# A new written order from the third batch on, other engines for movable operations, and squares taken from one SBUF copy

## The chip, the core and the metric

The kernel runs on one core of a Trainium2 chip. The core has TensorE (PE in the rows; its weight loads are PEld), VectorE (DVE), ScalarE (ACT), GpSimd (POOL) and SyncE (SP, which only starts transfers here). The metric is the device time of one execution in microseconds (us), as the median of several runs. "Slower" and "faster" are meant in this time.

## The reference

Cut to what matters:

```python
# attention: x (8, 8, 512, 64), state (8, 8, 32, 64)
scores  = scale * x @ state.T;   a  = softmax(scores)
xread   = a @ state
scores2 = scale * state @ x.T;   a2 = softmax(scores2)
sread   = a2 @ x
attn    = concatenate([xread, sread], axis=2)        # (8, 8, 544, 64)
# feed-forward on tokens of width 512, d_ff = 2048
h   = maximum(attn_as_tokens @ w_in, 0)
out = (h * h) @ w_out
```

Everything is float32. There are 8 batches of 512 read tokens and one last group of 256 tokens (the `sread` rows of all batches).

## The kernel before, in words

**Precision.** TensorE multiplies rounded float32 (`F32R`). Each operand is split into a rounded part (`hi`, made by ScalarE) and a remainder (`lo`, a subtraction), and a product is three matmuls: hi·hi, hi·lo, lo·hi.

**Blocks.** Block 0 to 7 is a batch, block 8 the `sread` tokens. For each block, `hidden(blk, fc)` computes 128 of the 2048 hidden features for all tokens into a PSUM bank `ph` (two banks in all), and `accumulate(blk, fc)` multiplies the squared result into four PSUM banks `acc`. Between the two, ScalarE and VectorE make `g_hi` and `g_lo` of the squared relu. A PSUM bank `ph` is free again only when `g_lo` has been made from it, so TensorE can wait twice for a late `g_lo`: in `accumulate`, which reads it, and in the hidden step two further on, which needs the bank.

The weights of `hidden` are not `w_in` but `w_in` already multiplied with the batch's `state` (`w2`). They are computed in rows of small matmuls (`w2ps`, `w4ps`), and scores (`st`) and reads (`pr`) stand in such rows too. For the last two batches `last_w2` splits `w2ps` into `w2h` (ScalarE) and `w2l` (VectorE). The softmax of each batch gives `k_hi`, `k_lo`.

**Blocks 5 to 7** use a product with seven instead of eight multiplications (`hidden_fast`, `accumulate_fast`, keys `fast.blk.p.h`). It needs sums of four quarters of the squares. Each step makes: `f_sum` (128x256), `d_sum` (128x256), `e_sum` (128x128), and the remainders `p_lo`, `f_lo` (tiles `a_g_lo`, 128x256) and `b_lo` (tile `b_g_lo`, 128x384). These are the small additions. `add_weights` (key `sums.p`) makes the matching sums of `w_out` (tiles `v`, `sv`, `one`, `both`, `first`); it runs beside the end of block 8 and all of block 5.

**What sets the order.** Nothing is scheduled at build time: a table of words, `PLAN`, is read from the start, each word lets one step go on to its next `yield`, and the engines get their instructions in exactly that order (`held` is never cleared). Each engine works its queue in order. A second table, `SECOND`, names the operations that go to the second of two engines: `pick(key, a, b)` gives `b` for a named key. For `d_sum`, `e_sum`, `f_sum`, `p_lo`, `f_lo`, `b_lo`, `sv` and `sv_lo` the second engine is GpSimd; for `w2_lo`, `wf_lo`, `k_lo`, `sm_sub`, `sm_mul` it is VectorE. A named `square.blk.fc` takes the square of blocks 0 to 4 and 8 on ScalarE instead of VectorE.

In `hidden`, a named square was three ScalarE instructions on the PSUM bank itself (relu `ph<-ph`, square `ph<-ph`, rounding `g_hi<-ph`). An unnamed one was relu to an SBUF tile (`r<-ph`), VectorE's product `ph<-ph,r`, and ScalarE's `g_hi<-r`.

Of the kernel before, what the change touches and what calls it, by code (L numbers as in the profile page):

```python
# [122 lines left out]
        accumulate.1.15 accumulate.1.15 load.3.1 load.3.1 hidden.2.1 hidden.2.1 accumulate.2.0 hidden.2.1
        split_wf.4 exp_s.2.1 hidden.2.1 hidden.2.1 hidden.2.1 exp_s.2.0 exp_s.2.0 transposes.2 split_wf.5
        later_w2.4 split_wf.5 later_w2.4 transposes.2 later_w2.4 later_w2.4 later_w2.4 later_w2.4 load_wf.1.6
        load_w2.2.2 load_w2.2.2 load_w2.2.3 later_w2.4 later_w2.4 later_w2.4 accumulate.2.1 later_w2.5 later_w2.5
        later_w2.5 hidden.2.2 later_w2.5 later_w2.5 prep.3.0 load.4.1 hidden.2.2 hidden.2.2 hidden.2.2 hidden.2.2
        hidden.2.2 load_wf.1.7 load.3.1 load.3.1 transposes.2 transposes.2 hidden.2.3 hidden.2.3 sread.1
        accumulate.2.2 hidden.2.3 hidden.2.3 hidden.2.3 hidden.2.3 later_w2.5 load_n.2.0 later_w2.5 later_w2.5
        hidden.2.5 split_wf.6 split_wf.6 split_wf.6 split_wf.6 hidden.2.5 later_w2.5 hidden.2.5 hidden.2.5  # L130
        load_w2.2.3 load_w2.2.3 hidden.2.5 hidden.2.5 load_w2.2.4 transposes.2 hidden.2.4 hidden.2.4 hidden.2.4
        hidden.2.4 hidden.2.4 hidden.2.4 accumulate.2.3 prep.3.1 load_n.2.1 split_wf.7 later_w2.6 later_w2.6
        later_w2.6 split_wf.7 split_wf.7 split_wf.7 accumulate.2.4 hidden.2.7 later_w2.6 load_w2.2.4 load_w2.2.4
        later_w2.6 later_w2.6 load_w2.2.5 load_wf.2.1 accumulate.2.5 later_w2.6 later_w2.6 later_w2.6 hidden.2.7
        hidden.2.7 hidden.2.7 hidden.2.7 hidden.2.7 later_w2.7 later_w2.7 load.4.1 load.4.1 later_w2.7 later_w2.7
        later_w2.7 later_w2.7 hidden.2.6 hidden.2.6 hidden.2.6 load.4.1 hidden.2.6 hidden.2.6 hidden.2.6 hidden.2.8
        hidden.2.8 hidden.2.8 hidden.2.8 hidden.2.8 hidden.2.8 load_w2.2.5 read.2 sread.2 load_w2.2.5
        accumulate.2.6 later_w2.7 later_w2.7 later_w2.7 sread.2 load_w2.2.6 sread.2 w2.1+scores.3 last_w2.1 start.5
        start.5 prep.4.0 last_w2.1 last_w2.1 last_w2.1 last_w2.1 transposed_scores.3.0 softmax.3.0 exp_s.3.0
        load_w2.2.7 load_w2.2.6 load_wf.2.0 accumulate.2.7 start.5 start.5 hidden.2.9 hidden.2.9 hidden.2.9  # L140
        load.5.1 load.5.1 transposed_scores.3.1 exp_s.3.1 load.5.1 hidden.2.9 accumulate.2.8 last_w2.1 load.5.1
        softmax.3.0 hidden.2.9 hidden.2.9 softmax.3.1 softmax.3.1 prep.4.1 hidden.2.10 exp_s.3.0 hidden.2.11
        exp_s.3.1 exp_s.3.1 hidden.2.10 hidden.2.10 exp_s.3.0 transposes.3 transposes.3 hidden.2.10 hidden.2.11
        hidden.2.10 hidden.2.10 accumulate.2.9 hidden.2.11 hidden.2.11 load_w2.2.6 softmax.3.1 hidden.2.11
        hidden.2.11 softmax.3.1 load_w2.2.7 load_n.3.0 softmax.3.0 softmax.3.0 softmax.3.0 softmax.3.0
        w2.0+scores.4 last_w2.0 transposed_scores.4.0 load_w2.2.7 last_w2.0 last_w2.0 last_w2.0 last_w2.0 last_w2.0
        softmax.3.0 softmax.3.0 accumulate.2.10 exp_s.4.0 prep.5.1 load_w2.3.0 prep.5.0 hidden.2.12 hidden.2.12
        hidden.2.12 exp_s.4.0 hidden.2.12 exp_s.4.0 hidden.2.13 hidden.2.13 load_n.3.1 start.6 start.6 hidden.2.13
        hidden.2.13 transposes.3 transposes.3 hidden.2.12 hidden.2.12 softmax.3.1 softmax.3.1 softmax.3.1
        accumulate.2.11 hidden.2.14 hidden.2.14 load_w2.3.1 load_w2.3.2 load_wf.2.2 transposed_scores.4.1 exp_s.4.1  # L150
        softmax.4.0 load_w2.3.0 exp_s.4.1 softmax.3.1 accumulate.2.12 softmax.4.1 exp_s.4.1 softmax.4.0 softmax.4.0
        hidden.2.13 hidden.2.13 hidden.2.14 transposes.3 hidden.2.15 hidden.2.14 hidden.2.14 hidden.2.14
# [1430 lines left out]
```

## Time and profile before

| what | value |
|---|---|
| median of 3 runs | 654.53 us (654.33 to 655.85) |
| the profiled execution's own time | 655.29 us |
| span of its instructions | 653.5 us, so 1.8 us lie around it |
| TensorE busy | 636.3 us (97%), 4453 matmul records |
| VectorE busy | 458.3 us (70%), 883 instructions |
| ScalarE busy | 403.6 us (62%), 835 instructions |
| GpSimd busy | 206.7 us (32%), 196 instructions |
| granted TensorE clock | 0.999 |

TensorE is busy in 39 of 40 slices, so what the kernel can win lies in TensorE's few waits and at its two ends. All instructions carry one line of the source (L419, a recording helper), so the rows are told apart by tile names. A number such as `5.7.1` in a name is block, pair and half.

### The profile page before, as it was taken

The numbers are of one execution on the slowest core, as the hardware profiler recorded it, in microseconds if no ns is written. First come the engines' busy times: TensorE is split into PE (matmuls) and PEld (weight loads), VectorE is DVE, ScalarE is ACT, GpSimd is POOL, SyncE is SP. The second block draws the span as 40 slices with busy tenths as digits, with TensorE's granted clock in tenths as the row PEclk, the third lists the DMA queues.
The fourth block names the chain that finished last, engine by engine and source line by source line (L and its number), as shares of the span: only waits on it lengthen the run. The fifth ranks groups of instructions, "written<-read, shape, count | busy, mean of one in ns | idle before, by whom it ended". The sixth has DMA issues, their size and how long they took to land.

```text
span 653.5 us, 12292 instructions
## 1 busy us (share of the span) xinstructions
PE 636.3 (97%) x4453; PEld 527.2 (81%) x4453; DVE 458.3 (70%) x883; ACT 403.6 (62%) x835; POOL 206.7 (32%) x196
## 2 busy tenths in 40 slices
...
GB/s 289 291 260 300 241 264 260 306 248 236 228 260 233 272 227 204 175 195 199 228 289 219 178 110 31 160 89 50 34 49 105 74 161 65 65 66 130 64 1 66
DMA packets 153132, 113.07 MB, mean 173 GB/s; under 512 B 93168, under 2 KB 126448, under 8 KB 153072
## 3 DMA queue, kind: packets, MB, share of 16 engines
...
q8 instruction: 35, 0.57, 0.4%
...
## 4 chain that ended last, share of the span: by engine, by line
PE 78%; DVE 10%; ACT 4%; issue 3%; DMA 2%; POOL 1%; SPq 0%; POOLq 0%; DVEq 0%; ACTq 0%
PE acc L419 32%; PE ph L419 24%; PE m L419 13%; PE w2ps L419 3%; PE w4ps L419 2%; PE pr L419 1%; ACT ph L419 1%; PE st L419 1%; DVE g_lo L419 1%; DVE m L419 1%; DVE v L419 1%; DMA w2a_d<-w2h 1%; PE pw L419 1%; DMA a<-a_d 1%; DMA xn<-in_x_dram 1%
## 5 line engine op out<-in xcount | busy, mean ns | idle before, releaser
L419 PE MATMUL acc<-wo,g_hi 128*128 128x512 f32 x704 | 203.8, 393 | 0.0
L419 PE MATMUL ph<-k_hi,w 128*128 128x512 f32 x512 | 176.6, 394 | 3.9 <-ACT w4o L419 1.3
L419 PEld LDWEIGHTS acc<-wo,g_hi 128*128 128x128 f32 x704 | 130.7, 188 | 33.0 <-ACT w2h L419 2.5
L419 PE MATMUL acc<-wo,g_lo 128*128 128x512 f32 x352 | 122.5, 392 | 1.2 <-DVE g_lo L419 1.1
L419 PEld LDWEIGHTS ph<-k_hi,w 128*128 128x128 f32 x512 | 96.2, 188 | 27.7 <-issue 2.7
L419 PE MATMUL ph<-k_lo,w 128*128 128x512 f32 x256 | 100.3, 392 | 0.0
L419 ACT ACTIVATE ph<-ph 128x512 f32<-128x512 f32 (+1 forms) x124 | 68.3, 551 | 49.3 <-PE ph L419 43.7
L419 DVE TENSOR_TENSOR g_lo<-ph,g_hi 128x512 fp32r<-128x512 f32 (+1 forms) x95 | 60.5, 640 | 48.5 <-ACT g_hi L419 46.7
L419 PEld LDWEIGHTS acc<-wo,g_lo 128*128 128x128 f32 x352 | 65.7, 188 | 17.4 <-DVE g_lo L419 3.0
L419 ACT ACTIVATE r<-ph 128x512 f32<-128x512 f32 (+1 forms) x82 | 47.5, 580 | 43.7 <-PE ph L419 41.8
L419 PEld LDWEIGHTS ph<-k_lo,w 128*128 128x128 f32 x256 | 48.2, 188 | 8.0
L419 POOL TENSOR_TENSOR sp<-sp,m 128x512 f32<-128x512 f32 x17 | 18.8, 1108 | 76.1 <-DVE m L419 69.4
L419 POOL TENSOR_TENSOR w<-w_f,w 128x512 fp32r<-128x512 f32 x17 | 23.3, 1368 | 59.7 <-ACT w L419 46.4
L419 ACT CAST g_hi<-ph 128x512 fp32r<-128x512 f32 (+1 forms) x62 | 34.3, 553 | 2.3 <-PE acc L419 0.9
L419 POOL TENSOR_TENSOR wf<-wf,wf_hi 128x512 fp32r<-128x512 f32 x10 | 13.3, 1333 | 62.4 <-ACT wf_hi L419 52.0
L419 DVE SCALAR_TENSOR_TENSOR ph<-ph,r 128x512 f32<-128x512 f32 (+1 forms) x34 | 21.8, 643 | 14.8 <-ACT r L419 14.6
L419 ACT CAST w<-w_f 128x512 fp32r<-128x512 f32 x40 | 24.6, 619 | 7.5 <-DMA w_f<-w_d 7.5
L419 DVE TENSOR_TENSOR w<-w_f,w 128x512 fp32r<-128x512 f32 x23 | 17.1, 749 | 16.2 <-ACT w L419 16.1
L419 POOL TENSOR_SCALAR dec<-wo_raw 128x512 f32<-128x512 f32 x10 | 20.8, 2087 | 12.8 <-DMA wo_raw<-in_moe_w_out_dram 12.7
L419 ACT ACTIVATE g<-r 128x512 f32<-128x512 f32 x35 | 21.8, 629 | 0.6
L419 ACT ACTIVATE g_hi<-r 128x512 fp32r<-128x512 f32 (+1 forms) x34 | 20.0, 593 | 3.0 <-PE acc L419 2.5
L419 ACT COPY w4o<-w4ps 128x512 f32<-128x512 f32 x21 | 11.9, 588 | 14.8 <-PE w4ps L419 14.2
...
## 6 DMA issues: line engine op xcount, KB each, us to landing
...
```

The source lines that it names most:

```text
L419: op = call(*args, **kw)
```

## The change

The order of `PLAN` is new from the third batch on; what stands ahead of it is the same. The keys of `SECOND` are new too: 96 of the small additions and remainders of blocks 5 to 7 stood on GpSimd, 69 do now. And in blocks 2 to 4 and 8 the relu now always goes to the SBUF tile `r`; a named square then reads `r` and writes `ph`, and `g_hi` is always made from `r`.

```diff
-        softmax.2.1 softmax.2.1 start.3 start.4 split_wf.5 start.3 softmax.2.1 hidden.1.15 hidden.1.15 split_wf.5
...
+        softmax.2.1 softmax.2.1 start.3 start.4 split_wf.5 start.3 softmax.2.1 hidden.1.15 hidden.1.15 split_wf.4
...
 SECOND = """
-    d_sum: 5.3.0 5.4.0 6.0.0 6.1.0 6.1.1 6.2.1 6.4.0 6.5.1 6.6.0 7.0.1 7.1.1 7.3.0 7.4.0 7.4.1 7.5.0 7.5.1 7.6.0
+    d_sum: 5.6.1 6.0.0 6.0.1 6.3.1 7.1.0 7.1.1 7.2.1 7.4.1 7.5.0 7.5.1
...
-    sm_mul: 3.0 3.1 4.1 5.0 5.1 6.0 6.1 7.0
+    sm_mul: 3.0
...
@@ in hidden(blk, fc, nt)
-        if square in second:
+        if square in second and blk < NX:
             nc.scalar.activation(ph, ph, AF.Relu)
         else:
             r = p2.tile([P, nt], F32, tag="g", name=f"r{blk}_{fc}", bufs=2)
             nc.scalar.activation(r, ph, AF.Relu)
         yield
-        if chosen(square):
+        if blk < NX and square in second:
             nc.scalar.activation(ph, ph, AF.Square)
+        elif blk >= NX and chosen(square):
+            nc.scalar.activation(ph, r, AF.Square)
         else:
             nc.vector.scalar_tensor_tensor(ph, ph, 0.0, r, ALU.max, ALU.mult)
         yield
```

What this makes of the engines' queues: TensorE has the same 3839 matmuls, VectorE 44 instructions more (885 to 929), GpSimd 24 fewer (201 to 177), ScalarE 20 fewer (823 to 803). Transfers are the same in number and size. On VectorE there are 27 more of the small ones of blocks 5 to 7, 14 more products for squares, 5 more copies of `w4ps` and 8 fewer softmax products. On GpSimd the large operations (128x512) rise by 8 softmax products and 4 `w2` remainders, and fall by 2 each of `wf` and `k_lo`.

Three places follow, each with the queue before and after.

The first is VectorE at the start of block 4: `g_lo4_1` is the remainder that the second `accumulate` of the block waits for; `w2_4_2` is a remainder of a weight, `sp6`, `aT6` and `m16` belong to batch 6's softmax, `o3` to the output of block 3.

```order
L419 TENSOR_REDUCE m16_0_4007<-sp6_0_3879 128x16
L419 TENSOR_SCALAR m16_0_4007<-m16_0_4007 128x16
L419 RECIPROCAL m16_0_4007<-m16_0_4007 128x16
L419 TENSOR_TENSOR sp6_0_3879<-sp6_0_3879,m16_0_4007 128x512
L419 STREAM_TRANSPOSE aT6_0_4134<-sp6_0_3879 128x512
L419 TENSOR_TENSOR w2_4_2_3826<-w2_f4_2_3827,w2_4_2_3826 128x2x256
L419 TENSOR_TENSOR sp6_1_3897<-sp6_1_3897,m16_1_3991 128x512
L419 TENSOR_TENSOR g_lo4_1_4122<-ph4_1_4114,g_hi4_1_4121 128x512
```

```order
L417 TENSOR_TENSOR w2_4_2_4022<-w2_f4_2_4023,w2_4_2_4022 128x2x256
L417 SCALAR_TENSOR_TENSOR ph4_0_4097<-ph4_0_4097,r4_0_4106 128x512
L417 TENSOR_TENSOR g_lo4_0_4105<-ph4_0_4097,g_hi4_0_4104 128x512
L417 COPY o3_1_4142<-acc3_0_1_3282 128x512
L417 COPY o3_3_4151<-acc3_0_3_3284 128x512
L417 SCALAR_TENSOR_TENSOR ph4_2_4112<-ph4_2_4112,r4_2_4121 128x512
L417 TENSOR_TENSOR g_lo4_2_4120<-ph4_2_4112,g_hi4_2_4119 128x512
L417 SCALAR_TENSOR_TENSOR ph4_1_4156<-ph4_1_4156,r4_1_4181 128x512
L417 TENSOR_TENSOR g_lo4_1_4180<-ph4_1_4156,g_hi4_1_4179 128x512
```

The softmax and weight work no longer stands directly ahead of `g_lo4_1`. On TensorE, a row of `w2ps` and `st` matmuls now stands between the first and the second `accumulate` of block 4, where before the second followed at once.

The second is VectorE in block 2, at a row of `w2ps` matmuls that takes both `ph` banks: they are free again after `w2l0_0` and `w2l0_1`, and the next hidden step waits for the first of them.

```order
L419 TENSOR_TENSOR g_lo2_11_2912<-ph2_11_2891,g_hi2_11_2911 128x512
L419 TENSOR_REDUCE m13_1_2877<-sp3_1_2851 128x16
L419 TENSOR_SCALAR m13_1_2877<-m13_1_2877 128x16
L419 RECIPROCAL m13_1_2877<-m13_1_2877 128x16
L419 TENSOR_REDUCE m13_0_2807<-sp3_0_2805 128x16
L419 TENSOR_SCALAR m13_0_2807<-m13_0_2807 128x16
L419 RECIPROCAL m13_0_2807<-m13_0_2807 128x16
L419 TENSOR_TENSOR sp3_0_2805<-sp3_0_2805,m13_0_2807 128x512
L419 STREAM_TRANSPOSE aT3_0_2943<-sp3_0_2805 128x512
L419 STREAM_TRANSPOSE sp4_0_2976<-st4_0_2947 128x512
L419 TENSOR_TENSOR w2l0_0_2974<-w2ps0_6_0_2945,w2h0_0_2973 128x512
```

```order
L417 TENSOR_TENSOR g_lo2_12_2957<-ph2_12_2949,g_hi2_12_2956 128x512
L417 TENSOR_REDUCE m13_1_2939<-sp3_1_2881 128x16
L417 TENSOR_SCALAR m13_1_2939<-m13_1_2939 128x16
L417 RECIPROCAL m13_1_2939<-m13_1_2939 128x16
L417 TENSOR_REDUCE m13_0_2943<-sp3_0_2845 128x16
L417 TENSOR_SCALAR m13_0_2943<-m13_0_2943 128x16
L417 RECIPROCAL m13_0_2943<-m13_0_2943 128x16
L417 TENSOR_TENSOR sp3_0_2845<-sp3_0_2845,m13_0_2943 128x512
L417 TENSOR_TENSOR w2l0_0_3016<-w2ps0_6_0_2987,w2h0_0_3015 128x512
L417 TENSOR_TENSOR w2l0_1_3022<-w2ps0_6_1_2988,w2h0_1_3021 128x512
L417 STREAM_TRANSPOSE aT3_0_3037<-sp3_0_2845 128x512
L417 STREAM_TRANSPOSE sp4_0_3040<-st4_0_2989 128x512
```

The two transposes now stand behind `w2l0_0` and `w2l0_1` instead of ahead of them.

The third is TensorE where block 5 ends and block 6 begins (`ph6_n` is hidden step n of block 6, the `m` tiles are the sums of block 5).

```order
L419 MATMUL m76_5_1_5376<-both7_5954,b_g_lo5.7.1_6172 128x256
L419 MATMUL ph6_1_6220<-k_hi6_6115,w2_6_0_5998 128x512
L419 MATMUL ph6_1_6220<-k_lo6_6116,w2_6_0_5998 128x512
L419 MATMUL ph6_1_6220<-k_hi6_6115,w2_6_0_5998 128x512 x2
L419 MATMUL ph6_1_6220<-k_lo6_6116,w2_6_0_5998 128x512
L419 MATMUL ph6_1_6220<-k_hi6_6115,w2_6_0_5998 128x512
L419 MATMUL ph6_2_6254<-k_hi6_6115,w2_6_1_6000 128x512
```

```order
L417 MATMUL m76_5_1_5383<-both6_5806,b_g_lo5.6.1_6181 128x256
L417 MATMUL ph6_3_6245<-k_hi6_6066,w2_6_1_6165 128x512
L417 MATMUL ph6_3_6245<-k_lo6_6067,w2_6_1_6165 128x512
L417 MATMUL ph6_3_6245<-k_hi6_6066,w2_6_1_6165 128x512 x2
L417 MATMUL ph6_3_6245<-k_lo6_6067,w2_6_1_6165 128x512
L417 MATMUL ph6_3_6245<-k_hi6_6066,w2_6_1_6165 128x512
L417 MATMUL m34_5_1_5381<-wo14_1646,a_g_hi5.7.1_6204 128x256 x2
```

Before, step 5.7.1 ran to its end and then four hidden steps (6.1 to 6.4) stood in a row ahead of the first sums of block 6. Now the hidden steps 6.0, 6.1, 6.3, 6.2 and 6.5 stand singly between the groups of 5.7.0, 5.6.1, 5.7.1 and 6.0.0.

## Rows read from the trace of the kernel before

**Rows 1.** The page, part 1: busy time, share of the span, instructions of each engine.

```profile
PE 636.3 (97%) x4453; PEld 527.2 (81%) x4453; DVE 458.3 (70%) x883; ACT 403.6 (62%) x835; POOL 206.7 (32%) x196
```

**Rows 2.** Busy time by stretch: PE, PEld, DVE, ACT, POOL, clock, DMA share, GB/s.

```profile
240.00:400.00 160.00, 157.94 (x1181) 124.38 (x1182) 101.68 (x194) 87.37 (x170) 31.44 (x25) 1.00 0.71 196
...
440.00:520.00 80.00, 78.69 (x502) 70.28 (x500) 74.68 (x159) 59.16 (x138) 24.39 (x23) 1.00 0.21 64
520.00:540.00 20.00, 19.15 (x122) 16.81 (x121) 14.17 (x28) 11.79 (x27) 8.58 (x12) 1.00 0.42 132
```

**Rows 3.** Timeline of PE, an undisturbed place: start, length, what, count.

```profile
309.60 0.39 PE L419 MATMUL ph<-k_hi,w 128*128 128x512 f32 x1
309.83 0.39 PE L419 MATMUL ph<-k_lo,w 128*128 128x512 f32 x1
```

**Rows 4.** Timeline of PE at the start of block 4.

```profile
344.11 0.61 PE L419 MATMUL acc<-wo,g_hi 128*128 128x512 f32 x2
345.84 0.50 PE L419 MATMUL acc<-wo,g_lo 128*128 128x512 f32 x1 [1.11 <-DVE g_lo L419]
346.17 0.62 PE L419 MATMUL acc<-wo,g_hi 128*128 128x512 f32 x2
```

**Rows 5.** Timelines of ACT, POOL and DVE at the same place.

```profile
341.84 0.59 ACT L419 CAST g_hi<-ph 128x512 fp32r<-128x512 f32 x1
...
343.03 1.60 POOL L419 TENSOR_TENSOR w<-w_f,w 128x512 fp32r<-128x512 f32 x1 [19.76 <-ACT w L419]
...
343.40 1.78 DVE L419 TENSOR_TENSOR sp<-sp,m 128x512 f32<-128x512 f32 x1
345.10 0.68 DVE L419 TENSOR_TENSOR g_lo<-ph,g_hi 128x512 fp32r<-128x512 f32 x1
```

**Rows 6.** Timelines of PE and DVE in block 2, around the row of `w2ps0`.

```profile
240.25 0.47 PE L419 MATMUL ph<-k_hi,w 128*128 128x512 f32 x1 [1.11 <-DVE w2l L419]
...
234.82 1.08 DVE L419 TENSOR_SCALAR m<-m 128x16 f32<-128x16 f32 x1
...
238.00 0.71 DVE L419 STREAM_TRANSPOSE aT<-sp 128x512 f32<-128x512 f32 x1
...
239.45 1.25 DVE L419 TENSOR_TENSOR w2l<-w2ps,w2h 128x512 fp32r<-128x512 f32 x2
```

**Rows 7.** Timeline of PE where block 5 ends and block 6 begins.

```profile
519.75 0.40 PE L419 MATMUL m<-two_first,b_g_hi5.7.1_6171 128*128 128x256 f32 x2
...
520.68 0.41 PE L419 MATMUL m<-both,b_g_hi5.7.1_6171 128*128 128x256 f32 x2
...
528.77 0.40 PE L419 MATMUL m<-first,b_g_hi6.0.0_6290 128*128 128x256 f32 x2
529.66 0.39 PE L419 MATMUL m<-first,b_g_lo6.0.0_6291 128*128 128x256 f32 x1 [0.48 <-POOL b_g_lo6.0.0_6291 L419]
529.88 0.39 PE L419 MATMUL ph<-k_hi,w 128*128 128x512 f32 x1
```

**Rows 8.** Timeline of PE at its last step, 7.7.1.

```profile
644.00 0.28 PE L419 MATMUL m<-both,b_g_lo7.7.0_7693 128*128 128x256 f32 x1
...
645.49 0.40 PE L419 MATMUL m<-wo,a_g_hi7.7.1_7685 128*128 128x256 f32 x2
```

**Rows 9.** ACT by form: count, busy us, mean ns, idle before and its releaser.

```profile
L419 ACT ACTIVATE ph<-ph 128x512 f32<-128x512 f32 x104 | 60.9, 586 | 46.4 <-PE ph L419 43.7 <-ACT w4o L419 0.9
L419 ACT ACTIVATE r<-ph 128x512 f32<-128x512 f32 x76 | 45.3, 596 | 42.3 <-PE ph L419 41.8
...
L419 ACT ACTIVATE g_hi<-r 128x512 fp32r<-128x512 f32 x28 | 17.5, 630 | 2.0 <-PE acc L419 1.5
```

**Rows 10.** Timeline of DVE between 440 and 520: stretched, ordinary, stretched.

```profile
441.02 1.05 DVE L419 TENSOR_TENSOR sv<-v 128x512 f32<-128x512 f32 x1
...
463.98 0.42 DVE L419 TENSOR_TENSOR s5.0.1_5377<-g 128x256 f32<-128x256 f32 x1
...
517.31 0.96 DVE L419 TENSOR_TENSOR s5.7.1_6118<-g 128x256 f32<-128x256 f32 x1
```

More of the change, by code (lines that the diff above doesn't have):

```diff
@@ L123 @@
[L123 to L152, printed above, removed]
@@ new lines @@
+        hidden.2.9 hidden.2.7 hidden.2.7 hidden.2.7 hidden.2.7 hidden.2.7 hidden.2.7 read.2 sread.2 hidden.2.8
+        sread.2 later_w2.7 sread.2 load_w2.2.6 accumulate.2.7 hidden.2.8 hidden.2.8 hidden.2.8 hidden.2.8
+        hidden.2.8 load_w2.2.5 load_w2.2.5 load_wf.2.0 w2.1+scores.3 last_w2.1 last_w2.1 later_w2.7 load.4.1
+        accumulate.2.8 start.5 start.5 start.5 start.5 transposed_scores.3.0 exp_s.3.0 load_w2.2.7 last_w2.1
+        last_w2.1 load_w2.2.6 load_w2.2.6 last_w2.1 last_w2.1 exp_s.3.0 exp_s.3.0 prep.4.1 hidden.2.11 hidden.2.11
@@ new lines @@
+        accumulate.2.13 prep.5.0 transposed_scores.4.1 hidden.2.14 hidden.2.14 load_w2.3.1 exp_s.4.1 start.6
+        softmax.4.1 hidden.2.15 hidden.2.15 hidden.2.15 exp_s.4.1 softmax.4.1 exp_s.4.0 hidden.3.0 softmax.4.1
+        softmax.4.1 softmax.4.1 accumulate.2.14 accumulate.2.15 exp_s.4.1 exp_s.4.0 transposes.4 softmax.4.0
+        load.6.1 load.6.1 load.6.1 transposes.4 hidden.3.0 hidden.3.0 accumulate.2.15 accumulate.2.15 hidden.3.0
+        accumulate.2.15 accumulate.2.15 accumulate.2.15 accumulate.2.15 softmax.4.0 softmax.4.0 load.6.1 hidden.3.1
@@ new lines @@
+        load_w2.3.6 w2.2+scores.5 last_w2.2 transposed_scores.5.0 transposed_scores.5.1 transposes.4 last_w2.2
+        last_w2.2 last_w2.2 last_w2.2 exp_s.5.0 accumulate.3.2 exp_s.5.0 hidden.3.4 hidden.3.5 hidden.3.4
+        hidden.3.4 hidden.3.4 prep.6.1 exp_s.5.1 exp_s.5.0 accumulate.3.3 exp_s.5.1 load_n.4.1 start.7 start.7
+        start.7 load_w2.3.4 load_w2.3.5 load_w2.3.4 softmax.5.0 exp_s.5.1 hidden.3.4 hidden.3.4 hidden.3.5
+        last_w2.2 prep.6.0 hidden.3.5 load_w2.3.7 hidden.3.5 hidden.3.5 hidden.3.5 load_wf.2.3 start.7
```

434 lines of the change are left out of this document (225 added, 209 removed), and 3 rows, old and new, of the table SECOND.

## The prediction

> **What bounds the kernel now.** I read the page first: TensorE is busy 97% of the span, the next engine 70% [rows 1]. The matmuls are the same before and after, so the only things that can change the time are the places where TensorE waits. The table of stretches says where they are: from 240 to 400 us TensorE is idle 160 − 157.94 = 2.06 us, from 440 to 520 1.31 us, from 520 to 540 0.85 us [rows 2]. VectorE is busy 74.68 of 80 us in the middle one, 101.68 of 160 in the first: it is crowded only while `add_weights` runs beside blocks 8 and 5.
>
> A wait costs more than the idle time beside it. Undisturbed, matmuls of 512 columns start 0.23 us apart although each is shown as 0.39 us long [rows 3], so up to 0.16 us of a gap hides under the matmul before it, and the first matmul after a wait takes longer. At the start of block 4 four starts in a row run from 344.11 to 346.17, 2.06 us where three steps of 0.23 would be 0.68: the wait cost 1.38 us, with 1.11 us of it shown as idle [rows 4]. So I price a wait at its idle time plus 0.27 us. From the one at 240.25 [rows 6] to the one at 529.66 [rows 7] the timeline has 14 waits with 5.26 us of idle time together: 5.26 + 14 × 0.27 = 9.0 us. The last step adds 1.0 us: its starts run from 644.00 to 645.49, 1.49 us for four matmuls [rows 8], which take 0.12 us each (two in a row last 0.40, one 0.28). About 10 us is therefore all that a better order can win behind the unchanged start.
>
> **The change, part by part.** *The wait at 345.84.* `g_hi` was ready at 341.84 + 0.59 = 342.43, but `g_lo` began only at 345.10: VectorE first had to do a weight's remainder and a softmax subtraction that took 1.78 us beside GpSimd's 1.60 us remainder [rows 5]. In the new queue the square and `g_lo4_1` follow directly on block 4's own operations, and TensorE has a row of small matmuls more to do before it needs them. What was late is ready before; the softmax pieces that stood in front are done earlier or on GpSimd, where nobody waits for them at once. I take the whole 1.4 us.
>
> *The wait at 240.25.* It is of the same size, 1.11 us idle [rows 6], so 1.4 us. VectorE reached `w2l` only at 239.45, behind a scaling of 128x16 that took 1.08 us and two transposes that ran from 238.00 to 239.45 [rows 6]. The new order puts both transposes behind `w2l`: 1.45 us sooner, more than the 1.11 that was missing. 1.4 us.
>
> *The border of blocks 5 and 6.* Three matmuls from 519.75 to 520.68 took 0.93 us instead of 0.36; three from 528.77 to 529.88 took 1.11 [rows 7]: 0.57 and 0.75 us lost. The new order puts hidden steps singly between the groups, so each chain of sums has a hidden step of 6 × 0.23 = 1.4 us more of cover. But `b_lo6.0.0`, which ended the second wait, stays on GpSimd. I take the first whole and two thirds of the second: 1.1 us.
>
> *The last step.* Three groups of 21 matmuls stand ahead of 7.7.1 as before, in another order (7.7.0 now before 7.6.1), and fewer GpSimd operations run beside VectorE. I take half of 1.0 us: 0.5 us.
>
> *The other waits.* Those three cost 1.38 + 1.38 + 0.57 + 0.75 = 4.1 of the 9.0 us; some 4.9 us lie in ten or so short waits whose surroundings are all written anew. Bounds: all gone, or as many again. I have no row that says which, and take a fifth off: 1.0 us.
>
> *Small additions back to VectorE.* 27 of them leave GpSimd: 18 of 256 columns, 8 of 128, one of 384. An ordinary one of 256 takes 0.42 us [rows 10] and starts about 0.34 after the one before; the 27 come to about 8 us of VectorE. Most fall behind 540 us, beside idle time of VectorE, and cost nothing; were VectorE full there, they would cost the 8 us. In the crowded stretch the count hardly grows: from `g_lo8_15` to the end of 5.7.1 VectorE has 139 instructions before and 145 after, 56 us of starts both times. But what runs beside GpSimd there is stretched: 15 instructions between 441.02 and 517.31 took 0.68 to 1.26 us instead of 0.4 to 0.7, some 6 us together [rows 10], beside 23 GpSimd instructions [rows 2]. About 13 of the 23 are left, so some 3 us of stretching goes. Against that, VectorE gets 11 instructions more (about 5 us) between `g_lo8_8` and `g_lo8_15`. Net for the crowded stretch between a gain of 3 and a loss of 5 us; I take a loss of 0.9 us.
>
> *Large operations on GpSimd.* In blocks 2 to 4 it gets about 8 more of 1.1 to 1.6 us. One of those stretched a subtraction from 0.69 to 1.78 us [rows 5], which was the longest wait of all. The Trainium skill, "SBUF — State Buffer", section "Who interferes with whom", says that a VectorE instruction with two SBUF inputs and a GpSimd instruction that reads SBUF exclude each other, each for the whole length of the other. By that rule eight more could hold VectorE for up to 8 × 1.3 = 10 us, an estimate. The trace agrees in kind (1.78 us beside 1.60). My sum goes by rows: one wait of 1.38 us came of 25 GpSimd instructions in that stretch [rows 2, 4], so eight more give 8 × 1.38 / 25 = 0.4 us. Between 0 and 8 × 1.38 = 11 us, I take 0.4 us.
>
> *Squares through `r`.* Before, a named square was relu, square and rounding of 0.586, 0.586 and about 0.59 us; now 0.596 for `r`, then a form that the trace lacks (square of SBUF into PSUM, between 0.586 and 0.630, I take 0.630), then `g_hi<-r` with 0.630 [rows 9]: 0.1 us more on ScalarE for each of 28. ScalarE is idle 46.4 us in front of `ph<-ph` alone, waiting for TensorE [rows 9], which hides it; uncovered it would be 2.8 us. Fourteen squares go over to VectorE, where a product can run beside `g_hi`; in blocks 2 to 4 that has 58 us to spare [rows 2].
>
> **Sum.** −1.4 − 1.4 − 1.1 − 0.5 − 1.0 + 0.9 + 0.4 = −4.1 us. The profiled execution took 655.29 us, 0.76 above the median of the runs, so the profile after should read about 651.2 and the median 654.53 − 4.1 = 650.4 us.
>
> **The rivals.** About 0.3% (2 us) is what this measurement tells from no change.
>
> *As many new waits as old ones go.* A written order only moves waits: the queues are in order, and each piece of softmax or weight work that leaves the front of one `g_lo` stands in front of another. For it: all of ScalarE's and VectorE's work still has to pass, and VectorE has 44 instructions more. Against it: at the two longest waits the queue shows what replaces them. It gives −1.4 − 1.4 + 1.4 × 2 = 0: 654.5 us, between 652.6 and 656.5.
>
> *VectorE becomes the bound in blocks 8 and 5 (slower).* From `g_lo8_8` to the end of step 5.5.1 it gets 158 instructions instead of 143, about 65 instead of 60 us of starts, where it is 93% busy [rows 2]. If the stretching does not fall with the GpSimd instructions, the 5 us show in full and half of them again as waits of 0.27 us each in some ten places: −1.4 − 1.4 + 5 + 2.7 = +4.9, so 659.4 us; it decides once VectorE is busy more than about 97% between 440 and 520 us. Against it: 10 GpSimd instructions fewer beside it. The Trainium skill speaks for this rival: "Perfetto Trace Analysis", section "Optimizing Scalar/DVE Operations", advises to offload a saturated VectorE, even to GpSimd, with the caution that the two share a port; the change does the reverse. The 93% agree that it is nearly saturated there, the stretched rows that the caution holds.
>
> *Nearly all waits go.* The new order may cover the ten short waits as it covers the long ones: −9.0 − 1.0 + 1.3 = −8.7, so 645.8 us. For it: each is short (0.27 us idle on average). Against it: the same VectorE load in the crowded stretch.
>
> **How the numbers follow.** My forecast (647.5 to 652.5 us) has 0.48, nearly all waits gone 0.14, as many new as old 0.22, VectorE as the bound 0.16. Faster by over 0.3% is 0.48 + 0.14 = 0.62, within 0.3% 0.21, slower 0.17 with the upper edge of the case of new waits. The range that leaves out no more than 2 in 10 reaches from 646.5 to 656.5 us; the likeliest sign alone has 647.5 to 652.5.
>
> **What will show it.** In the profile after, TensorE's idle time from 240 to 400 us should fall from 2.06 to under 1 us, with no wait of over 1 us at a `g_lo` of block 4 or at a `w2l` of block 2. From 520 to 540 us it should fall under 0.4 us. VectorE between 440 and 520 us should stay near 75 of 80 us busy with fewer stretched instructions, GpSimd fall to about 14 us there. `ph<-r` should last 0.59 to 0.63 us. Wrong would be: a new wait of over 1 us in blocks 2 to 4 beside a large GpSimd operation, or TensorE idle over 2 us between 440 and 520 us.

## The result and the profile after

The changed kernel takes 646.55 us (median of 4 runs, 644.39 to 647.50) against 655.16 us of the kernel before in the same runs: a ratio of 0.9864, 95% interval [0.9835, 0.9894], so about 8.9 us less. The forecast was 650.4 us, 4.1 us less: right in its sign, and less than half of the size; the result lies at the very edge of the wider range, 646.5 to 656.5 us. The profiled execution took 646.96 us, its span is 645.1 us.

Page, part 1, of the changed kernel, to hold against [rows 1]:

```profile
PE 631.9 (98%) x4453; PEld 528.1 (82%) x4453; DVE 465.8 (72%) x927; ACT 394.7 (61%) x815; POOL 184.5 (29%) x172
```

Busy time by stretch in the changed kernel (columns as in [rows 2]: PE, PEld, DVE, ACT, POOL, clock, DMA share, GB/s):

```profile
240.00:400.00 160.00, 160.00 (x1225) 127.12 (x1210) 108.71 (x207) 86.95 (x167) 38.70 (x33) 1.00 0.75 206
...
440.00:520.00 80.00, 79.16 (x511) 71.82 (x510) 72.91 (x172) 62.76 (x143) 13.06 (x15) 1.00 0.22 70
520.00:540.00 20.00, 20.00 (x141) 18.74 (x140) 15.60 (x35) 10.86 (x24) 5.10 (x6) 1.00 0.37 119
```

From 240 to 400 us and from 520 to 540 us TensorE does not wait at all, where before it was idle 2.06 and 0.85 us [rows 2]. VectorE did not get fuller between 440 and 520 us: 72.91 us instead of 74.68, with 13 more instructions, while GpSimd went from 24.39 us in 23 instructions to 13.06 in 15.

The two profiled executions did not start alike. Up to a group of four `acc<-wo,g_lo` at about 173 us the program is the same in both kernels. TensorE's timeline has this group and the last matmul of all, first in the kernel before, then in the changed one:

```profile
172.97 1.07 PE L419 MATMUL acc<-wo,g_lo 128*128 128x512 f32 x4
...
647.51 0.28 PE L419 MATMUL m<-both,b_g_lo7.7.1_7730 128*128 128x256 f32 x1
```

```profile
174.87 1.07 PE L417 MATMUL acc<-wo,g_lo 128*128 128x512 f32 x4
...
639.53 0.28 PE L417 MATMUL m<-both,b_g_lo7.7.1_7770 128*128 128x256 f32 x1
```

The changed kernel came to the common group 1.90 us later, though nothing of the change stands ahead of it: in the 14 profiled executions of this document that place is reached between 171.73 and 174.87 us. From there to the last matmul the kernel before takes 474.54 us and the changed one 464.66, so 9.9 us less. Behind the last matmul 0.4 us more are gone.

TensorE's waits between 175 and 632 us (who waited, for whom; us in total, times, longest; the smallest groups are not listed), first of the kernel before:

```profile
PE ph L419 <- ACT w4o L419: 1.3, 2, 0.7
PE acc L419 <- DVE g_lo L419: 1.1, 1, 1.1
PE ph L419 <- DVE w2l L419: 1.1, 1, 1.1
PE ph L419 <- DVE g_lo L419: 1.1, 3, 0.4
...
```

and of the changed kernel, all that is listed:

```profile
PE ph L417 <- DVE g_lo L417: 1.2, 3, 0.6
PE w4ps L417 <- DVE g_lo L417: 1.0, 1, 1.0
```

The whole list of before has 6.3 us in 12 waits, that of after 2.2 us in 4. The prediction's "ten or so short waits" are gone almost to the last. Three of the starts that still come late, in the timeline of the changed kernel, with what GpSimd and VectorE do ahead of the second:

```profile
195.77 0.38 PE L417 MATMUL w4ps<-wf_hi,s 64*128 64x256 f32 x1 [1.05 <-DVE g_lo L417]
...
444.27 0.94 PE L417 MATMUL ph<-sr_k_hi,s 128*128 128x512 f32 x4 [0.61 <-DVE g_lo L417]
...
441.89 1.35 POOL L417 TENSOR_TENSOR sv<-v 128x512 f32<-128x512 f32 x1 [2.56 <-DVE both L417]
442.25 1.54 DVE L417 TENSOR_TENSOR w<-w_f,w 128x512 fp32r<-128x512 f32 x1 [0.17 <-ACT w L417]
...
636.29 0.51 PE L417 MATMUL m<-two_first,b_g_hi7.7.1_7769 128*128 128x256 f32 x2 [0.48 <-ACT b_g_hi7.7.1_7769 L417]
636.92 0.39 PE L417 MATMUL m<-two_first,b_g_lo7.7.1_7770 128*128 128x256 f32 x1
```

The last step still waits, 0.61 us instead of 0.48: 0.48 in front of the start at 636.29, and 0.13 ahead of that at 636.92. The new form of ScalarE, by form (count, busy us, mean ns), is a little shorter than the 630 ns that were assumed:

```profile
L417 ACT ACTIVATE ph<-r 128x512 f32<-128x512 f32 x20 | 12.0, 602 | 0.5
```

### The profile page after: what moved, and what is told of

Its sections match the earlier page's. It is cut to its first block, busy times and chain, and to the rows that moved or that the text cites. A ratio compares the mean times of both kernels' runs of the same rounds, so it can differ in the third digit from the quotient of the medians.

```text
span 645.1 us, 12288 instructions
## 1 busy us (share of the span) xinstructions
PE 631.9 (98%) x4453; PEld 528.1 (82%) x4453; DVE 465.8 (72%) x927; ACT 394.7 (61%) x815; POOL 184.5 (29%) x172
## 4 chain that ended last, share of the span: by engine, by line
PE 94%; DVE 2%; issue 1%; DMA 1%; ACT 1%; SPq 0%; POOLq 0%; POOL 0%; DVEq 0%; ACTq 0%
PE acc L417 37%; PE ph L417 30%; PE m L417 18%; PE w2ps L417 3%; PE w4ps L417 2%; PE pr L417 1%; PE st L417 1%; PE pw L417 1%; DMA xn<-in_x_dram 1%; PE px L417 1%; DVE g_lo L417 1%; DVE ph L417 0%; PE pst L417 0%; ACT r L417 0%; PE pa L417 0%
## 5 line engine op out<-in xcount | busy, mean ns | idle before, releaser
L417 ACT ACTIVATE r<-ph 128x512 f32<-128x512 f32 (+1 forms) x124 | 70.4, 569 | 97.8 <-PE ph L417 92.6
L417 DVE SCALAR_TENSOR_TENSOR ph<-ph,r 128x512 f32<-128x512 f32 (+1 forms) x48 | 31.1, 648 | 42.3 <-ACT r L417 42.1
L417 POOL TENSOR_TENSOR w<-w_f,w 128x512 fp32r<-128x512 f32 x21 | 28.9, 1383 | 74.1 <-ACT w L417 37.9
L417 POOL TENSOR_TENSOR sp<-sp,m 128x512 f32<-128x512 f32 x25 | 26.6, 1067 | 72.3 <-DVE m L417 67.5
L417 ACT ACTIVATE g_hi<-r 128x512 fp32r<-128x512 f32 (+1 forms) x76 | 44.0, 582 | 4.9 <-PE acc L417 3.8
L417 POOL TENSOR_TENSOR wf<-wf,wf_hi 128x512 fp32r<-128x512 f32 x8 | 10.9, 1367 | 67.9 <-ACT wf_hi L417 67.9
L417 ACT ACTIVATE ph<-ph 128x512 f32<-128x512 f32 x40 | 23.5, 587 | 10.1 <-PE ph L417 8.6
L417 DVE TENSOR_REDUCE m<-sp 128x16 f32<-128x512 f32 x28 | 18.7, 670 | 3.3 <-ACT sp L417 3.1
L417 POOL TENSOR_TENSOR s<-sf,s 128x512 fp32r<-128x512 f32 x6 | 7.8, 1292 | 43.3 <-ACT s L417 43.3
L417 ACT COPY w4o<-w4ps 128x512 f32<-128x512 f32 x16 | 9.1, 588 | 13.8 <-PE w4ps L417 9.7
```

What stands on the lines that cost most here:

```text
L417: op = call(*args, **kw)
```

## The experiments

All kernels were timed against the kernel before. The fourth column is the list of waits as above, with its total and count. The last one is the time from the common group at about 173 us to the last matmul, and in brackets what this is more or less than before. It leaves the start out, but it is one execution of each kernel, so half a microsecond in it says little.

| kernel | median, us | ratio to before | TensorE's waits, 175 to 632 us | common group to last matmul, us |
|---|---|---|---|---|
| changed | 646.55 | 0.9864 [0.9835, 0.9894] | 2.2 us, 4 | 464.66 (−9.9) |
| new order alone | 655.65 | 0.9993 [0.9976, 1.0009] | 6.5 us, 11 | 475.26 (+0.7) |
| new engines alone | 661.39 | 1.0080 [1.0054, 1.0106] | 11.9 us, 17 | 480.06 (+5.5) |
| changed, square code as before | 646.43 | 0.9848 [0.9824, 0.9872] | 2.6 us, 5 | 465.10 (−9.4) |
| changed, small additions as before | 648.68 | 0.9880 [0.9858, 0.9902] | 3.0 us, 5 | 468.05 (−6.5) |
| changed, engines of squares as before | 648.71 | 0.9904 [0.9869, 0.9938] | 3.2 us, 8 | 468.10 (−6.4) |
| changed, large operations as before | 648.35 | 0.9885 [0.9861, 0.9910] | 4.0 us, 6 | 467.57 (−7.0) |
| changed, remaining group as before | 647.42 | 0.9869 [0.9845, 0.9892] | 3.6 us, 6 | 466.86 (−7.7) |
| new order, small additions and code of the squares new, all else as before | 652.26 | 0.9951 [0.9936, 0.9966] | 5.8 us, 10 | 472.43 (−2.1) |
| before, two waits mended | 656.08 | 1.0004 [0.9988, 1.0019] | 5.8 us, 13 | 474.52 (0.0) |
| changed, ten remainders 3.05 us late | 676.54 | 1.0317 [1.0286, 1.0348] | | 495.53 (+21.0) |
| changed, ten remainders 1.83 us late, one 0.61 | 660.75 | 1.0072 [1.0046, 1.0097] | | 478.88 (+4.3) |
| changed, two waits mended | 646.07 | 0.9851 [0.9820, 0.9883] | 1.7 us, 3 | 464.77 (−9.8) |

### The new order alone, the new engines alone

The kernel before with the new `PLAN`:

```diff
 PLAN = """
...
-        softmax.2.1 softmax.2.1 start.3 start.4 split_wf.5 start.3 softmax.2.1 hidden.1.15 hidden.1.15 split_wf.5
+        softmax.2.1 softmax.2.1 start.3 start.4 split_wf.5 start.3 softmax.2.1 hidden.1.15 hidden.1.15 split_wf.4
...
```

> The kernel before with the new written order alone; engines and squares as before. Theory A (the order took the waits behind 175 us away, whichever engines do the movable work): 646.5 to 649.5 us, at most 2 us of the 8.6 lost, TensorE's idle time behind 175 us under 3.5 us instead of the 7 of before. Rival B (fewer and shorter collisions of VectorE with GpSimd are the gain): above 652 us. Rival C (order and engines fit only each other): at or above before, 655 to 660 us, with new waits of over 0.5 us at sums that VectorE or GpSimd now makes at the wrong place.

The kernel before with the new `SECOND`:

```diff
 SECOND = """
-    b_lo: 5.6.1 6.0.0 6.0.1 6.2.1 6.3.0 6.5.0 6.6.0 6.7.0 7.2.1 7.4.0
+    b_lo: 5.6.1 6.0.0 6.1.1 6.4.1 6.5.0 7.0.0 7.0.1 7.1.0 7.4.1
...
-    sm_mul: 3.0 3.1 4.1 5.0 5.1 6.0 6.1 7.0
+    sm_mul: 3.0
...
```

> The kernel before with the new choice of engines alone; order and squares as before. Theory A: no gain, 654 to 658 us: the long waits at 240 and 345 us stay, and VectorE, with more instructions in the crowded stretch from 440 to 520 us, makes some waits there longer. Rival B: 649 to 652 us, since 27 small additions fewer are on GpSimd and VectorE is stretched less. Rival C: slower than before, 657 us or more.

Measured: the order alone gives nothing (0.9993), the engines alone cost 5 us (1.0080), both together save 8.9. Theory A falls by the order alone, B by the engines alone; C holds, though the new waits stand at `g_lo` and not at sums. The order alone does take the long waits from 240 to 400 us away (TensorE is busy 159.07 of 160 there), but other waits stand elsewhere. Its waits:

```profile
PE ph L419 <- DVE g_lo L419: 3.9, 7, 1.1
PE w4ps L419 <- DVE g_lo L419: 2.1, 3, 1.3
...
```

One of them costs far more than its idle time. Timeline of TensorE at that place, and the stretch behind it:

```profile
195.56 0.38 PE L419 MATMUL w4ps<-wf_hi,s 64*128 64x256 f32 x1 [1.34 <-DVE g_lo L419]
...
196.59 1.22 PE L419 MATMUL acc<-wo,g_hi 128*128 128x512 f32 x2
```

```profile
196.00:200.00 4.00, 4.00 (x18) 3.09 (x15) 2.58 (x5) 1.07 (x2) 0.00 (x0) 0.57 0.92 273
```

Two matmuls of 512 columns take 1.22 us instead of 0.61 [rows 4], and the granted clock is 0.57 over 4 us: for most of them TensorE ran at the lower of its two levels, 1.2 instead of 2.4 GHz. That is 4 × 0.43 = 1.7 us. The worst wait of the engines alone is longer, without that:

```profile
342.09 0.50 PE L417 MATMUL ph<-k_hi,w 128*128 128x512 f32 x1 [2.06 <-DVE g_lo L417]
```

```profile
338.00:344.00 6.00, 3.94 (x17) 2.72 (x16) 3.82 (x8) 2.95 (x7) 0.13 (x1) 1.00 0.95 313
```

### One part of the change undone

The code of the squares as before, order and engines new:

```diff
-        if square in second and blk < NX:
+        if square in second:
             nc.scalar.activation(ph, ph, AF.Relu)
...
-        elif blk >= NX and chosen(square):
-            nc.scalar.activation(ph, r, AF.Square)
```

> The changed kernel with the squares as before (relu, square and rounding all on the PSUM bank). Theory A: within 1 us of the changed kernel, 645.5 to 647.5 us: the squares cost 0.1 us of ScalarE each, and ScalarE is 61% busy. Rival D (the SBUF copy sets the bank free earlier or saves reads of PSUM, and is part of the gain): 649 us or more.

Measured 646.43 us: the SBUF copy is worth nothing that can be told from no change. D falls.

The small additions of blocks 5 to 7 on the engines of before (the keys of `b_lo`, `d_sum`, `e_sum`, `f_lo`, `f_sum`, `p_lo`):

```diff
-    d_sum: 5.6.1 6.0.0 6.0.1 6.3.1 7.1.0 7.1.1 7.2.1 7.4.1 7.5.0 7.5.1
+    d_sum: 5.3.0 5.4.0 6.0.0 6.1.0 6.1.1 6.2.1 6.4.0 6.5.1 6.6.0 7.0.1 7.1.1 7.3.0 7.4.0 7.4.1 7.5.0 7.5.1 7.6.0
...
```

> The changed kernel with the small additions of blocks 5 to 7 on the engines of before (96 instead of 69 on GpSimd), all else new. Theory A: 646.5 to 649 us, the waits ahead of 440 us unchanged, at most some waits of 0.3 us in blocks 5 and 6. Rival B: 650 to 653 us, with VectorE stretched by about 23 us behind 440 us again instead of the 15 of the changed kernel and waits at most sums of block 5.

Measured 648.68 us, at the upper end of theory A: 2.1 us more than the changed kernel, 2.3 more than the kernel just above. The timelines show waits that the changed kernel hasn't, one behind a remainder on GpSimd, and longer than the 0.3 us that theory A allowed:

```profile
515.93 0.50 PE L412 MATMUL ph<-k_hi,w 128*128 128x512 f32 x1 [0.47 <-ACT r L412]
...
539.62 0.39 PE L412 MATMUL m<-wo,a_g_lo6.2.1_6505 128*128 128x256 f32 x1 [0.48 <-POOL a_g_lo6.2.1_6505 L412]
```

The squares of blocks 2 to 4 and 8 on the engines of before (88 keys of `square` instead of 74):

```diff
...
-        2.11 2.12 2.14 2.15 3.0 3.1 3.2 3.4 3.7 3.8 3.9 3.11 3.12 3.14 3.15 4.5 4.9 5.1 5.2 5.3 5.4 5.7 5.9 5.10
+        2.5 2.8 2.9 2.10 2.11 2.12 2.13 2.15 3.3 3.4 3.5 3.7 3.10 3.11 3.12 3.13 3.14 3.15 4.1 4.5 4.6 4.7 4.8
...
```

> The changed kernel, with the squares of blocks 2 to 4 and 8 given to ScalarE and VectorE as before (14 more of them on ScalarE). Theory S (a square on ScalarE makes the chain from the last matmul of a hidden step to its remainder some 0.5 us longer and holds ScalarE 0.6 us more, which shows where a row of small matmuls wants both banks at once): 649 to 653 us, TensorE's waits at 180 and 195 us near the 1.1 and 1.3 us of the run with the order alone. Theory L (the large remainders and softmax products matter, the squares don't): 646 to 648 us.

Measured 648.71 us, between the ranges of the two theories and closer to S. One of the places where it shows is hidden step 2.5, behind which a row of `w4ps` wants both `ph` banks. ScalarE, VectorE and TensorE there, with the square on ScalarE:

```profile
194.00 0.60 ACT L412 ACTIVATE r<-ph 128x512 f32<-128x512 f32 x1
194.63 0.60 ACT L412 ACTIVATE ph<-r 128x512 f32<-128x512 f32 x1
195.17 0.61 ACT L412 ACTIVATE g_hi<-r 128x512 fp32r<-128x512 f32 x1
...
195.81 0.69 DVE L412 TENSOR_TENSOR g_lo<-ph,g_hi 128x512 fp32r<-128x512 f32 x1 [1.05 <-ACT g_hi L412]
...
196.56 0.38 PE L412 MATMUL w4ps<-wf_hi,s 64*128 64x256 f32 x1 [1.35 <-DVE g_lo L412]
```

From relu to the remainder's start it takes 1.81 us, since ScalarE does three things in a row. In the changed kernel VectorE makes the product beside `g_hi`:

```profile
193.52 0.60 ACT L417 ACTIVATE r<-ph 128x512 f32<-128x512 f32 x1
194.15 0.63 ACT L417 ACTIVATE g_hi<-r 128x512 fp32r<-128x512 f32 x1
...
194.20 0.69 DVE L417 SCALAR_TENSOR_TENSOR ph<-ph,r 128x512 f32<-128x512 f32 x1
195.02 0.69 DVE L417 TENSOR_TENSOR g_lo<-ph,g_hi 128x512 fp32r<-128x512 f32 x1
```

That is 1.50 us, and TensorE waits 1.05 instead of 1.35. So theory S holds here, but this place makes up only 0.3 us of the loss, and the wait at about 181 us, which S expected near 1.1 us, is 0.34 as against 0.33. TensorE's matmuls stand in the same order in both kernels: counted from the common group, the matmul that starts at 220.65 us in the changed kernel starts 2.1 us later here. Most of the loss lies in such short delays between 182 and 221 us, the rest mainly in block 8; not each of them was followed to its square.

The large operations on the engines of before (`w2_lo`, `wf_lo`, `k_lo`, `sm_sub`, `sm_mul`):

```diff
-    sm_mul: 3.0
+    sm_mul: 3.0 3.1 4.1 5.0 5.1 6.0 6.1 7.0
...
-    wf_lo: 1.0 1.1 2.1 3.1 4.0 6.0 6.1 7.1
+    wf_lo: 1.0 1.1 2.1 3.1 4.1 5.0
```

> The changed kernel, with the large remainders (of w2, wf and k) and the softmax subtractions and products on the engines of before: 14 operations of 128x512 go back from GpSimd to VectorE, 4 the other way. Theory L (on VectorE they stand in front of a remainder that TensorE waits for; on GpSimd nobody waits for them): 649 to 653 us, with new waits of 0.5 to 1.2 us at g_lo in blocks 2 to 4. Theory S: 646 to 648 us. The Trainium skill's rule of the shared port read by itself would have it faster, 643 to 645 us, since 10 large GpSimd operations fewer hold VectorE up.

Measured 648.35 us, 1.8 us more than the changed kernel and between the ranges of the two theories; the waits that came up are those of theory L, and the gain that the expectation's last sentence has did not come. (Net of each kind, 12 operations go back, 8 of the softmax and 4 of `w2`, and 4 the other way, so GpSimd has 8 fewer, 164 instead of 172 instructions, and not 10.) Timelines of VectorE and TensorE at the two places where waits came up:

```profile
179.05 1.28 DVE L412 TENSOR_TENSOR wf<-wf,wf_hi 128x512 fp32r<-128x512 f32 x2
...
181.58 0.50 PE L412 MATMUL ph<-k_hi,w 128*128 128x512 f32 x1 [1.14 <-DVE g_lo L412]
...
258.93 0.69 DVE L412 TENSOR_TENSOR sp<-sp,m 128x512 f32<-128x512 f32 x1
...
263.16 0.50 PE L412 MATMUL ph<-k_hi,w 128*128 128x512 f32 x1 [0.74 <-DVE g_lo L412]
```

One of the two `wf` remainders was on GpSimd in the changed kernel, where the wait at 181.71 is 0.33 us; here VectorE has some 0.6 us more in front of `g_lo` and the wait is 0.81 longer. The softmax product of 0.69 us was on GpSimd too, and there is no wait at `g_lo3_0` then. VectorE is full at these places, though it is busy only 68% from 240 to 400 us: what it gets more goes straight into the wait.

The remaining group (`w4_out`, `out`, `sv`, `sv_lo`, `v`, `w_in_lo`, `g_sq`) as before:

```diff
-    w4_out: 0.1 1.3 2.2 3.1 3.3 4.0 4.1 4.2 5.0 6.0 6.1 6.2 6.3 7.1 7.2 7.3
+    w4_out: 0.1 1.3 2.2 3.1 3.3 5.1 5.3 6.0 6.3 7.0 7.1
...
```

> The changed kernel with the remaining group of movable operations (copies of w4ps and of outputs, sums and remainders of the output weights, squares of blocks 5 to 7) on the engines of before. If every group of engine choices is worth about 2 us with this order, as the small additions, the squares and the large operations were, 647.5 to 649 us. If this group costs what is missing between those three (some 6 us together) and the 9 us that the old engines cost in all: about 649.5 us. If it is worth nothing: 646.5 us.

Measured 647.42 us: 0.9 us by the medians, no difference by the ratios (0.9869 and 0.9864); in the profiled execution 2.2 us from the common group on. And the reverse of most of it: in the changed kernel all keys as before except those of the six small additions (the code of the squares stays new):

```diff
-    sm_mul: 3.0
+    sm_mul: 3.0 3.1 4.1 5.0 5.1 6.0 6.1 7.0
...
```

> The changed kernel with every movable operation on the engine of before except the small additions of blocks 5 to 7, which stay where the change puts them. If the groups simply add up, it is 2.1 us (what the small additions cost) below the run with the order alone, 653.5 us. If the gain needs the whole choice of engines together, it is at the run with the order alone or above, 655 us or more.

Measured 652.26 us, a ratio of 0.9951 against 0.9993 with the order alone: 2.8 us, where 2.1 was expected. By the medians the groups, taken out of the changed kernel one at a time, cost 2.1 (small additions), 2.2 (squares), 1.8 (large operations) and 0.9 us (the rest): 7.0 of the 9.1 us between the order alone and the changed kernel. By the last column they cost 3.4, 3.4, 2.9 and 2.2: 11.9 of 10.6. So with the new order the groups roughly add up, to within what these readings can tell. A single group is near the limit of the ratios: the interval of the changed kernel, 0.9835 to 0.9894, holds those of the runs without the small additions, the large operations and the rest.

### Two waits of the kernel before, mended by themselves

```diff
-        softmax.3.0 w2.0+scores.4 last_w2.0 transposed_scores.4.0 load_w2.2.7
-        last_w2.0 last_w2.0 last_w2.0 last_w2.0 last_w2.0
+        w2.0+scores.4 last_w2.0 load_w2.2.7
+        last_w2.0 last_w2.0 last_w2.0 last_w2.0 last_w2.0 softmax.3.0 transposed_scores.4.0
...
-        load_w2.4.2 hidden.4.3 hidden.4.1 load_w2.4.3 hidden.4.3 softmax.6.1 hidden.4.1 hidden.4.1
+        hidden.4.3 hidden.4.1 load_w2.4.3 hidden.4.3 hidden.4.1 hidden.4.1 load_w2.4.2 softmax.6.1
```

> The kernel before with two places of VectorE's queue reordered by hand and nothing else: the remainder g_lo4_1 goes ahead of a weight's remainder and a softmax product, w2l0_0 and w2l0_1 go ahead of two transposes. The prediction's price for both waits is 2 x 1.38 us: 2.8 us less than before in the same call. Rival: the work that is put off makes the next wait longer (the hidden step that reads the weight, the next softmax piece), and less than 1 us is gained.

Measured 1.0004 [0.9988, 1.0019], and no difference in the last column either: no gain of 2.8 us, the rival holds. Both waits are gone, and two new ones stand behind them. Timelines of VectorE and TensorE:

```profile
240.91 0.70 DVE L416 STREAM_TRANSPOSE aT<-sp 128x512 f32<-128x512 f32 x1
241.71 0.72 DVE L416 STREAM_TRANSPOSE sp<-st 128x512 f32<-128x512 f32 x1
...
243.22 2.49 DVE L416 STREAM_TRANSPOSE xT<-xp 128x512 f32<-128x512 f32 x4
...
246.48 0.65 DVE L416 TENSOR_TENSOR g_lo<-ph,g_hi 128x512 fp32r<-128x512 f32 x1
...
247.18 0.50 PE L416 MATMUL ph<-k_hi,w 128*128 128x512 f32 x1 [0.72 <-DVE g_lo L416]
...
349.65 0.67 PE L416 MATMUL w2ps<-wf,sT 64*32 64x256 f32 x16 [0.38 <-DVE g_lo L416]
```

The two transposes that went behind `w2l` stand now, with more of the same kind, in front of `g_lo2_12`, and VectorE works until then with pauses of at most 0.1 us. The time was handed on to the next remainder.

### What a wait costs

Ten remainders of the changed kernel were computed several times over, the same values again, so that they are late by a known time:

```diff
+            for _ in range(6 if (blk, fc) in LATE else 1):
+                nc.vector.tensor_sub(glo, ph, ghi.bitcast(F32))
-            nc.vector.tensor_sub(glo, ph, ghi.bitcast(F32))
```

with `LATE` = 3.3, 3.5, 3.7, 3.9, 3.12, 4.3, 4.5, 4.7, 4.9 and 4.12.

> The changed kernel with ten remainders g_lo of blocks 3 and 4 each computed six times over (the same values again), so that each is ready some 3.05 us later. If a wait costs what the timeline shows as idle plus 0.27 us, the time grows by the added idle time plus 0.27 us for each added wait, with about 10 waits 2.7 us more than the idle time alone; if a wait costs only what is shown idle, it grows by that alone. In size: slack of 0.5 to 2 us in front of each leaves 1 to 2.5 us each, so 657 to 672 us.

Measured 676.54 us, above the range. Busy time by stretch, 262 to 425 us:

```profile
262.00:425.00 163.00, 142.64 (x1078) 110.14 (x1077) 119.87 (x212) 70.86 (x137) 27.88 (x23) 0.95 0.59 168
```

TensorE was idle 20.36 us, but the granted clock was also only 0.95, which is 163 × 0.05 = 8.2 us. So the run was made again with four times instead of six, and `g_lo2_5` twice:

```diff
-            for _ in range(6 if (blk, fc) in LATE else 1):
+            for _ in range(LATE.get((blk, fc), 1)):
```

> The changed kernel with the same ten remainders of blocks 3 and 4 computed four times over (1.83 us later instead of 3.05), and g_lo2_5, which TensorE waits for 1.05 us at 195.77, twice (0.61 us later). Theory: with waits under some 2 us the granted clock stays at 1.00 and the time grows by the added idle time plus 0.27 us for each wait, so with ten waits of 0 to 2.6 us some 8 us of idle time and 10 to 11 us in all: 656 to 658 us. Rival (the clock also falls behind waits of 1.3 us, as it did at 195.56 in the run with the order alone): 2 us more for each such place, 660 us or more, and the window behind 196 us shows a clock of about 0.5.

Measured 660.75 us: the rival on the clock holds at two places. Three starts in TensorE's timeline, the waits between 280 and 410 us, the two stretches in which the clock was low, and the one behind them, in which it was not:

```profile
195.80 0.38 PE L417 MATMUL w4ps<-wf_hi,s 64*128 64x256 f32 x1 [1.77 <-DVE g_lo L417]
...
305.49 0.50 PE L417 MATMUL ph<-k_hi,w 128*128 128x512 f32 x1 [2.08 <-DVE g_lo L417]
...
457.76 0.47 PE L417 MATMUL ph<-sr_k_hi,s 128*128 128x512 f32 x1 [0.61 <-DVE g_lo L417]
```

```profile
PE pr L417 <- DVE g_lo L417: 4.3, 3, 1.5
PE ph L417 <- DVE g_lo L417: 3.9, 4, 2.1
PE ph L417 <- DVE w L417: 0.3, 1, 0.3
```

```profile
196.00:202.00 6.00, 6.00 (x27) 4.79 (x26) 2.13 (x4) 1.56 (x3) 0.00 (x0) 0.72 0.99 321
306.00:310.00 4.00, 4.00 (x12) 3.13 (x12) 1.48 (x4) 1.23 (x2) 0.00 (x0) 0.57 0.97 260
310.00:360.00 50.00, 48.54 (x379) 37.49 (x377) 36.83 (x71) 26.05 (x51) 7.89 (x7) 1.00 0.74 225
```

In the last stretch lies a wait of 1.46 us (328.32), and yet the clock stayed at 1.00, so not every wait of 1.3 us costs it. The first and the last of the three matmuls start at 195.77 and 444.27 in the changed kernel. From the first to the last it takes 248.50 us there and 261.96 here, 13.46 more. The eight waits have 8.5 us of idle time; the clock costs 6 × 0.28 + 4 × 0.43 = 3.4. What is left is 1.56 us, 0.2 for each wait. The prediction's price, idle time plus 0.27, was nearly right for waits behind which the clock stays up.

### Two waits of the changed kernel, mended

```diff
-        load_w2.5.1 load_w2.5.1 hidden.8.13 hidden.8.13
+        hidden.8.13 hidden.8.13 load_w2.5.1 load_w2.5.1
...
-    f_lo: 5.7.0 5.7.1 6.0.0 6.0.1 6.1.0 6.3.0 6.3.1 6.6.0 6.6.1 6.7.1 7.1.0 7.3.1 7.4.0 7.5.0 7.5.1 7.6.0 7.7.1
+    f_lo: 5.7.0 5.7.1 6.0.0 6.0.1 6.1.0 6.3.0 6.3.1 6.6.0 6.6.1 6.7.1 7.1.0 7.3.1 7.4.0 7.5.0 7.5.1 7.6.0
```

> The changed kernel with two of its last waits mended: g_lo8_13 goes ahead of a weight's remainder that took 1.54 us of VectorE beside GpSimd (wait of 0.61 us at 444.27), and the last f_lo goes from GpSimd to VectorE, so that the sum of 128x128 in front of the last rounding is not stretched to 0.83 us (wait of 0.48 us at 636.29). At idle time plus 0.27 us each: 0.9 + 0.7 = 1.6 us less, 645.0 us. Rival: the remainder is then late for the hidden step that reads it, or VectorE's own 0.42 us for the f_lo takes the place of the stretching: 646 to 647 us.

Measured 646.07 us, which can't be told from the 646.55 of the changed kernel. The wait at 444.27 is gone; the one at the last step only changed its cause (below). In the profiled execution TensorE also waits 0.41 us for a transfer at 316.80, which the edit does not touch, so a gain of half a microsecond can't be seen in it.

```profile
634.99 0.38 PE L409 MATMUL m<-two_first,b_g_lo7.7.1_7770 128*128 128x256 f32 x1 [0.47 <-DVE b_g_lo7.7.1_7770 L409]
```

## Why the prediction was right in sign and too small

**What bounds the kernel: right.** What was won came mostly out of TensorE's waits, as their list shows (6.3 us in 12, then 2.2 in 4). "About 10 us is therefore all that a better order can win behind the unchanged start" held too: 8.9 us by the medians, 9.9 from the common group on.

**The step that failed** is that on the other waits: "Bounds: all gone, or as many again. I have no row that says which, and take a fifth off: 1.0 us." They were worth 4.9 us by the prediction's price: ten waits with 2.2 us idle together (0.22 on average, not the 0.27 that the rival's text gives). Two are left, 0.23 us at 440.60 and 0.61 at 444.27 with 0.27 each, 1.4 us; so this term measured −3.5 instead of −1.0. The rival "Nearly all waits go" at 645.8 us, which got a chance of 0.14, is what happened. It was held down by "the same VectorE load in the crowded stretch"; in the run, the five waits of that stretch (1.31 us idle) became two (0.84 us), and VectorE's busy time fell by 1.8 us, with GpSimd at 13.06 us where about 14 was forecast. What the term had no place for is that these waits go only if order and engines change together: the list has 11 waits with the new order alone, 17 with the new engines alone and 4 with both.

**The stretch ahead of 240 us** was called an unchanged start. The new order begins at about 175 us, and four waits of before (1.46 us idle, 2.5 us by the prediction's price) were left out. The changed kernel has two there, 0.33 us at 181.71 and 1.05 at 195.77, 1.9 us: −0.6. The second is a new wait of over 1 us in block 2, but GpSimd does nothing beside it (0.00 us busy from 194 to 200 us), so it is not the one that the prediction named as a sign of being wrong. The short wait at 624.10 us of before (0.10 us idle) was left out too: −0.4.

**The waits at 345.84 and 240.25:** size right, 1.4 us each; between 240 and 400 us no idle time is left. The reason given was half of it. Moving the pieces that stand in front was enough to end those two waits, but not to win their time: done by itself it won nothing, since VectorE's queue handed the wait on. The whole order with other engines won it.

**The border of blocks 5 and 6:** −1.1 forecast, 0.57 + 0.75 = 1.3 gone.

**The last step:** −0.5 forecast, nothing won (0.61 us idle instead of 0.48).

**Small additions, +0.9, and large operations, +0.4:** neither cost showed. With the new order, putting either group back on its old engines costs 2.1 and 1.8 us by the medians, 3.4 and 2.9 from the common group on. Both have the opposite sign of their term. The Trainium skill, "SBUF — State Buffer", section "Who interferes with whom", is borne out for single instructions (1.54 us beside GpSimd's 1.35 us at 442.25, where a `w` remainder takes 0.68 us at 195.63). Here the 0.69 us that VectorE is spared in front of a remainder count for more. The Trainium skill, "Perfetto Trace Analysis", section "Optimizing Scalar/DVE Operations", says that offloading a saturated VectorE, even to GpSimd, may make sense; that is borne out by the large operations and not by the small additions (2.1 us better on VectorE).

**Squares:** the code costs nothing, as forecast, with 602 ns for the new form. That 14 of them went to VectorE was priced at nothing because ScalarE and VectorE have time to spare; it is worth 2.2 us by the medians. At hidden step 2.5, where TensorE stands and waits, the way from relu to the remainder is 0.3 us shorter; that the same holds at the other places, which make up most of the 2.2 us, is not shown.

**Sum.** −1.4 − 1.4 − 1.3 + 0.1 − 3.5 − 0.6 − 0.4 = −8.5. Of the 4.4 us between this and the forecast, 2.5 are the other waits, 1.3 the two costs that did not come and 1.0 the waits that were left out; the border adds 0.2 and the last step takes 0.6 back. That the two profiled executions differ by nearly as much, 655.29 − 646.96 = 8.3 us, is luck: the changed kernel had lost 1.9 us before the change begins, and won 9.9 behind it. So 1.4 us are named by no term. An estimate from the starts of all matmuls behind the common group, each held against the usual distance of its kind: the waits and the two starts behind each make 8.6 of the 9.9 us, and the other 1.2 are spread over starts that come a little late although no idle time is shown.

What is still open besides: which of the new places of the order and which single operations make the 14 us between "order 0, engines +5" and "both −8.9". The runs show that they need each other, and at a few places how.
